# The accumulating blocks of a two-stage expert MLP, with the products of the high parts written ahead of those of the low parts

## The chip, the cores and the metric

The kernel runs on one core of a Trainium2 chip. Its time is the device time of one execution in microseconds (us), the median of several executions. The engines are named as in the profile: PE multiplies matrices (PEld loads its weights), DVE, ACT and POOL work on vectors, SP issues transfers. POOL also issues the indirect transfers (gathers and scatters of rows).

## The reference

Three stages follow each other: a gated linear attention over 4 batches, 8 heads and 768 steps; a routed layer with 8 experts of 384 tokens each; and an MLP with an ELU. For a token `x` of expert `e`:

```python
h = np.maximum(x[mask] @ w1[e], 0.0)
out[mask] = h @ w2[e]
# and then, for all 3072 tokens
h = x @ w_in
g = np.where(h > 0.0, h, alpha * (np.exp(np.minimum(h, 0.0)) - 1.0))
return (g @ w_out)
```

The experts' hidden size is 1024, that of the last MLP is 2048, and a token has 320 numbers. Which expert takes which token is found by a greedy choice over all the scores, which the kernel computes expert after expert.

## The kernel before

The attention comes first. Then eight rounds follow, one for each expert (`NR = 8`), each with its 384 tokens. A round has four kinds of blocks on PE. `P1(r, f)` multiplies the tokens by 128 columns of the first expert matrix (eight blocks); `C1(r, f)` multiplies the result of `P1(r, f)` by the second expert matrix and adds it into three banks named `acc`; `P2(r, f)` does with `w_in` what `P1` does (sixteen blocks); `C2(r, f)` multiplies the result by `w_out` and adds it into three `acc` banks again, one for each 128 tokens. Block `f = 7` of `C1` and block `f = 15` of `C2` end their sums: ACT or DVE then copies the banks out, in `C1` as the input of `P2`, in `C2` as `ot`, which POOL scatters to the rows of the output (line 1375).

For accuracy every operand is a sum of a high and a low part. After a `P` block ACT or DVE writes the high part `gh` (lines 1240, 1093, 1095), and DVE subtracts to get the low part `gl` (lines 1247, 1100), which is therefore ready last. A `C2` block holds, for each of the three banks, three products: `gh` by the high weights (line 1362), `gh` by the low weights (1363) and `gl` by the high weights (1366). A `C1` block holds eight products, in the lines 1315 to 1332.

What stands where on an engine is decided when the program is built. `main` takes the blocks from a list; a `C` block stands some blocks behind its `P` block (`LAG = 3`). Each block is a generator; wherever it yields, side work may be inserted: the router of later rounds, the splitting of the next round's weights, and the transposes that bring the next round's tokens into shape (`prep_x`, line 1176; ACT writes their high part `xh`, and DVE their low part `xl` at line 1184). A planner (`Plan`) keeps an estimated time for each engine and from it decides what is inserted, and whether ACT or DVE takes a copy. Where the first `P1` block of a round comes before the planner has its tokens ready, `main` takes waiting `C2` blocks ahead of it.

One more line stands in the loop of `C2`: in the last round, at `f = 8` and the first bank, `nc.gpsimd.drain()` (line 1369) tells POOL to wait until what it has issued is finished; the planner books 8400 ns for it on POOL. The last `NL = 3` blocks of the last round are one call with `n = 3`.

Of the kernel before, what the change touches and what calls it, by code (L numbers as in the profile page):

```python
# [18 lines left out]
NR, CAP, TK = 8, 384, 384  # L19
# [889 lines left out]
class Mlp:  # L909
# [386 lines left out]
    def C1(self, r, f):  # L1296
        nc, PE, plan = self.nc, self.nc.tensor, self.plan
        A, V = nc.scalar, nc.vector
        if f == 0:
            self.ac = [self.acc.tile([128, 512], F32, name="acc") for _ in range(3)]  # L1300
        h, l, th, tl = self.take(r, 0, f)
        w = self.w2[:, f]
        e = f == 7
        if e:
            yh = self.pool.tile([128, 3, TK], F32R, name="yh", bufs=1)
            yl = self.pool.tile([128, 3, TK], F32R, name="yl", bufs=1)
            for _ in range(2):
                self.es.take(False)[0] = 1
            s = self.pool.tile([128, TK], F32, name="e", bufs=3)[:64]
            ys = self.pool.tile([128, TK], F32, name="e", bufs=3)  # L1310
            self.yst = (yh, yl)
        p = self.ac[2]
        plan.wait(th)
        if f == 0:
            PE.matmul(p[:, :TK], w[:, 512:640], h, start=True, stop=False)
        plan.wait(tl)
        PE.matmul(p[:64, :TK], w[:, 512:576], l, start=False, stop=False)  # L1317
        if f > 0:
            PE.matmul(p[:, :TK], w[:, 512:640], h, start=False, stop=e)  # L1319
        plan.pe(2, TK)  # L1320
        if e:
            A.activation(s, p[64:128, :TK], AF.Copy)
            t1 = plan.on("a", 488)
            V.tensor_tensor(ys[:64], p[:64, :TK], s, op=ALU.add)
            V.tensor_tensor(ys[64:], p[:64, :TK], s, op=ALU.add)
            plan.on("d", 1100, t1)
        for t in range(2):
            p = self.ac[t][:, :TK]
            c, cl = slice(t * 128, t * 128 + 128), slice(256 + t * 128, 384 + t * 128)
            PE.matmul(p, w[:, c], h, start=f == 0, stop=False)  # L1330
            PE.matmul(p, w[:, cl], h, start=False, stop=False)  # L1331
            PE.matmul(p, w[:, c], l, start=False, stop=e)  # L1332
            plan.pe(3, TK)
            if e:
                A.activation(yh[:, t], p, AF.Copy)  # L1335
                t1 = self.yready[t] = plan.on("a", 491)
                V.tensor_tensor(yl[:, t], p, yh[:, t], op=ALU.subtract)
                plan.on("d", 552, t1)
            else:
                yield  # L1340
        if e:
            A.activation(yh[:, 2], ys, AF.Copy)
            t1 = self.yready[2] = plan.on("a", 524)
            V.tensor_tensor(yl[:, 2], ys, yh[:, 2], op=ALU.subtract)
            plan.on("d", 552, t1)
            yield

    def C2(self, r, f, n=1):
        nc, PE, plan = self.nc, self.nc.tensor, self.plan
        if f == 0:  # L1350
            self.ac = [self.acc.tile([128, 512], F32, name="acc") for _ in range(3)]
        parts = {}
        idx = self.router.res[r][1]
        for t, f in [(t, f + i) for t in range(3) for i in range(n)]:
            if f not in parts:
                parts[f] = self.take(r, 1, f)
            h, l, th, tl = parts[f]
            c = slice(t * 128, t * 128 + 128)
            p = self.ac[t][:, :320]
            plan.wait(th)  # L1360
            wh, wl = self.wo(f)
            PE.matmul(p, h[:, c], wh, start=f == 0, stop=False)  # L1362
            PE.matmul(p, h[:, c], wl, start=False, stop=False)  # L1363
            plan.pe(2, 320)
            plan.wait(tl)
            PE.matmul(p, l[:, c], wh, start=False, stop=f == 15)  # L1366
            plan.pe(1, 320)
            if (r, t, f) == (NR - 1, 0, 8):
                nc.gpsimd.drain()
                plan.on("p", 8400)  # L1370
            if f == 15:
                o = self.pool.tile([128, 320], F32, name="ot", bufs=3)
                self.copy(o, p, 437, 490)
                nc.gpsimd.memset(self.spc, 0.0)
                s = nc.gpsimd.indirect_dma_start(out=self.out, out_offset=bass.IndirectOffsetOnAxis(ap=idx[:, t:t + 1], axis=0),  # L1375
                                                 in_=o, in_offset=None)
                for q in self.scat:
                    self.tc.declare_no_dep(s.ins, q.ins, reason="rows of other tokens")
                self.scat.append(s)
                plan.on("p", 1080)  # L1380
            yield
# [281 lines left out]
```

## Time and profile before

| what | value |
|---|---|
| median of 3 runs | 755.16 us (752.74 to 759.88) |
| profiled execution, its own time | 750.71 us |
| profiled execution, span | 748.9 us |
| PE busy in the span | 702.9 us (94%) |
| DVE busy in the span | 541.3 us (72%) |
| ACT busy in the span | 377.6 us (50%) |
| POOL busy in the span | 186.6 us (25%) |

The span runs from the first to the last instruction of the profiled execution; 1.8 us of its time lie around it. PE's share is that of a modelled end of each matmul, so gaps are better read from the starts of matmuls that follow each other. DRAIN and semaphore instructions are no busy time; they stand under an engine's queue (POOLq, SPq).

### The profile page before, as it was taken

To read this page: it belongs to the slowest core of one execution; us is meant where nothing else is said; L and a number is where in the kernel's file an instruction comes from. 1 tells how busy PE (TensorE), PEld (TensorE's weight loads), DVE (VectorE), ACT (ScalarE), POOL (GpSimd) and SP (SyncE) were. 2 spreads that over 40 slices of the span, in tenths; PEclk is the share of its full clock that TensorE was granted. 3 is DMA by queue.
4 is the path that set the end of the run, shared out by engine and by line. 5 is a ranking of instruction groups with operands and counts; after the bars stand their busy time and mean duration, and the time that the engine had idled before them with its cause. 6 is when DMAs were issued, how large, how long until landed. Compare 5 with 4: busy or idle time off the path is not lost.

```text
span 748.9 us, 17930 instructions
## 1 busy us (share of the span) xinstructions
PE 702.9 (94%) x7274; PEld 639.3 (85%) x7274; DVE 541.3 (72%) x1592; ACT 377.6 (50%) x804; POOL 186.6 (25%) x242
## 2 busy tenths in 40 slices
PE   7889888837999999999999999999999999999997
PEld 4656666626989999999999999999999999999997
DVE  8687888887898968965896698569868833851442
ACT  5455445435365725842772366256527743752443
POOL 5666655235111401210301120112022220001001
PEclk9899999957999999999999999999999999999999
DMA  7777968236002301400320230022013321100000
GB/s 280 237 231 226 251 212 261 51 109 214 18 1 85 124 1 51 131 28 1 103 80 28 85 93 5 27 85 98 1 30 109 112 88 45 36 1 26 1 2 27
DMA packets 22436, 67.31 MB, mean 90 GB/s; under 512 B 3536, under 2 KB 7632, under 8 KB 22352
## 3 DMA queue, kind: packets, MB, share of 16 engines
q1 hardware_dynamic: 14240, 35.12, 15.4%
q0 software_dynamic: 8064, 30.94, 12.4%
q8 instruction: 57, 0.93, 0.5%
q14 instruction: 27, 0.22, 0.1%
q10 hardware_dynamic: 48, 0.10, 0.0%
HBM read 58.28 MB, written 7.86 MB: 88 GB/s over the span
## 4 chain that ended last, share of the span: by engine, by line
PE 73%; issue 11%; DVE 9%; ACT 3%; POOL 2%; DMA 1%; POOLq 0%; SPq 0%; ACTq 0%; DVEq 0%
PE ph L1223 30%; PE acc L1362 6%; PE acc L1366 6%; PE acc L1363 6%; PE acc L1330 3%; PE acc L1332 3%; PE acc L1331 2%; PE pO L381 2%; PE pR L395 2%; PE pX L464 2%; PE acc L1317 1%; PE acc L1319 1%; PE pX L450 1%; PE pr L807 1%; PE pO L365 1%
## 5 line engine op out<-in xcount | busy, mean ns | idle before, releaser
L1276 DVE SCALAR_TENSOR_TENSOR e<-e,ph 128x384 f32<-128x384 f32 x128 | 70.3, 550 | 50.4 <-ACT e L1273 49.7
L1272 ACT ACTIVATE e<-ph 128x384 f32<-128x384 f32 x128 | 62.5, 488 | 79.4 <-PE ph L1223 74.3
L1223 PE MATMUL ph<-yh,wih 128*128 128x384 f32 x256 | 89.1, 348 | 0.7 <-DVE xl L1184 0.4
L1240 ACT ACTIVATE gh<-ph 128x384 fp32r<-128x384 f32 x64 | 31.3, 491 | 114.0 <-PE ph L1223 89.1
L1223 PE MATMUL ph<-yh,wil 128*128 128x384 f32 x256 | 86.1, 337 | 0.0
L1375 POOL DMA_INDIRECT out_dram<-ot,idx x24 | 24.0, 998 | 210.8 <-ACT ot L1093 207.8
L1100 DVE TENSOR_TENSOR gl<-e,gh 128x384 fp32r<-128x384 f32 x128 | 70.9, 561 | 1.8 <-ACT gh L1093 0.3
L1273 ACT ACTIVATE e<-e 128x384 f32<-128x384 f32 x128 | 67.3, 526 | 4.0
L1362 PE MATMUL acc<-woh,gh 128*128 128x320 f32 x216 | 68.3, 316 | 0.0
L1247 DVE SCALAR_TENSOR_TENSOR gl<-ph,gh 128x384 fp32r<-128x384 f32 x64 | 35.2, 552 | 45.5 <-ACT gh L1240 45.3
L1366 PE MATMUL acc<-woh,gl 128*128 128x320 f32 x216 | 66.9, 310 | 0.5 <-DVE gl L1100 0.5
L1363 PE MATMUL acc<-wol,gh 128*128 128x320 f32 x216 | 66.8, 309 | 0.0
L1223 PE MATMUL ph<-yl,wih 128*128 128x384 f32 x256 | 66.0, 338 | 0.0
L1093 ACT ACTIVATE gh<-e 128x384 fp32r<-128x384 f32 x96 | 49.0, 514 | 11.4 <-DVE e L1276 11.1
L1366 PE MATMUL acc<-woa,gl 128*128 128x320 f32 x168 | 52.4, 312 | 0.9 <-DVE gl L1100 0.9
L1362 PE MATMUL acc<-woa,gh 128*128 128x320 f32 x168 | 52.8, 314 | 0.0
L1223 PEld LDWEIGHTS ph<-yh,wih 128*128 128x128 f32 x256 | 48.1, 188 | 4.8 <-ACT yh L1335 4.1
L1363 PE MATMUL acc<-wob,gh 128*128 128x320 f32 x168 | 51.8, 308 | 0.0
L1223 PEld LDWEIGHTS ph<-yh,wil 128*128 128x128 f32 x256 | 48.1, 188 | 0.0
L1104 POOL DMA_INDIRECT stg<-in_w1a_dram,wi x16 | 15.7, 983 | 123.3 <-DVE wi L845 119.0
L1223 PEld LDWEIGHTS ph<-yl,wih 128*128 128x128 f32 x256 | 46.1, 188 | 0.0
L1223 PE MATMUL ph<-xh,w1h 128*128 128x384 f32 x128 | 44.6, 349 | 0.1
(290 smaller groups left out, 2041.4 us busy)
## 6 DMA issues: line engine op xcount, KB each, us to landing
vk<-in_vk_dram SPq DMA_DIRECT2D x24, 484.0 KB, 5.4
qk<-in_qk_dram SPq DMA_DIRECT2D x20, 320.0 KB, 5.5
cx<-in_win_dram SPq DMA_DIRECT2D x8, 512.0 KB, 5.1
xd<-x SPq DMA_DIRECT2D x48, 80.0 KB, 3.4
wx<-in_wout_dram SPq DMA_DIRECT2D x9, 320.0 KB, 3.0
cx<-in_wout_dram SPq DMA_DIRECT2D x5, 448.0 KB, 4.1
qk<-in_qk_dram SPq DMA_DIRECT2D x4, 512.0 KB, 6.1
cx<-in_win_dram SPq DMA_DIRECT2D x4, 256.0 KB, 5.7
```

The source lines that it names most:

```text
L1093: self.nc.scalar.activation(out, x, AF.Copy)
L1100: self.nc.vector.tensor_tensor(out, x, y, op=ALU.subtract)
L1223: PE.matmul(p, w, x, start=k == 0, stop=k == 7)
L1240: nc.scalar.activation(h, p, AF.Relu)
L1247: nc.vector.scalar_tensor_tensor(l, p, 0.0, h, op0=ALU.max, op1=ALU.subtract)
L1272: nc.scalar.activation(e, p, AF.Relu, scale=-1.0)
L1273: nc.scalar.activation(e, e, AF.Exp, scale=-1.0)
L1276: nc.vector.scalar_tensor_tensor(e, e, -1.0, p, op0=ALU.add, op1=ALU.max)
L1362: PE.matmul(p, h[:, c], wh, start=f == 0, stop=False)
L1363: PE.matmul(p, h[:, c], wl, start=False, stop=False)
L1366: PE.matmul(p, l[:, c], wh, start=False, stop=f == 15)
L1375: s = nc.gpsimd.indirect_dma_start(out=self.out, out_offset=bass.IndirectOffsetOnAxis(ap=idx[:, t:t + 1], axis=0), in_=o, in_offset=None)
```

## The change

In `C1`, the blocks `f = 0` to `6` now write five products with `gh` (lines 1316, 1318, 1319 of the changed program), a yield, the three with `gl` (1324, 1325), a yield, and return. In `C2`, the blocks `f = 0` to `14` that are called with `n = 1` write six products with `gh` over the three banks (1371, 1372), with yields after the fourth and the sixth, then the three with `gl` (1379), a yield, and return. The closing blocks (`f = 7`, `f = 15`) and the last call with `n = 3` keep the old order. The products themselves, 5730 matmuls in the program, are the same.

The early return of `C2` stands ahead of the line that drains POOL, and that line asks for `f = 8`; in the call with `n = 3`, `f` is 13, 14 or 15. The changed program has no such DRAIN left; the closing ones at the program's end (line 1659 before, 1689 now) are in both.

```diff
@@ C1
         p = self.ac[2]
         plan.wait(th)
-        if f == 0:
-            PE.matmul(p[:, :TK], w[:, 512:640], h, start=True, stop=False)
+        if not e:
+            q = [x[:, :TK] for x in self.ac]
+            PE.matmul(q[2], w[:, 512:640], h, start=f == 0, stop=False)
+            for t in range(2):
+                PE.matmul(q[t], w[:, t * 128:t * 128 + 128], h, start=f == 0, stop=False)
+                PE.matmul(q[t], w[:, 256 + t * 128:384 + t * 128], h, start=False, stop=False)
+            plan.pe(5, TK)
+            yield
+            plan.wait(tl)
+            for t in range(2):
+                PE.matmul(q[t], w[:, t * 128:t * 128 + 128], l, start=False, stop=False)
+            PE.matmul(q[2][:64], w[:, 512:576], l, start=False, stop=False)
+            plan.pe(3, TK)
+            yield
+            return
         plan.wait(tl)
         PE.matmul(p[:64, :TK], w[:, 512:576], l, start=False, stop=False)
-        if f > 0:
-            PE.matmul(p[:, :TK], w[:, 512:640], h, start=False, stop=e)
+        PE.matmul(p[:, :TK], w[:, 512:640], h, start=False, stop=e)
@@ C2
         parts = {}
+        if n == 1 and f < 15:
+            h, l, th, tl = self.take(r, 1, f)
+            wh, wl = self.wo(f)
+            plan.wait(th)
+            q = [(x[:, :320], slice(t * 128, t * 128 + 128)) for t, x in enumerate(self.ac)]
+            for t, (p, c) in enumerate(q):
+                PE.matmul(p, h[:, c], wh, start=f == 0, stop=False)
+                PE.matmul(p, h[:, c], wl, start=False, stop=False)
+                plan.pe(2, 320)
+                if t == 1:
+                    yield
+            yield
+            plan.wait(tl)
+            for p, c in q:
+                PE.matmul(p, l[:, c], wh, start=False, stop=False)
+            plan.pe(3, 320)
+            yield
+            return
         idx = self.router.res[r][1]
```

On PE, the first `C2` block of the first round. Before (a row names the line, the operation and what it writes from what; a bracket names whom it waits for):

```order
L1223 MATMUL ph<-yl,wis 128x384
L1362 MATMUL acc<-woa,gh 128x320 [waits DVE_49]
L1363 MATMUL acc<-wob,gh 128x320
L1366 MATMUL acc<-woa,gl 128x320 [waits DVE_49]
L1362 MATMUL acc<-woa,gh 128x320
L1363 MATMUL acc<-wob,gh 128x320
```

Now:

```order
L1223 MATMUL ph<-yl,wis 128x384
L1371 MATMUL acc<-woa,gh 128x320 [waits DVE_49]
L1372 MATMUL acc<-wob,gh 128x320
L1371 MATMUL acc<-woa,gh 128x320
L1372 MATMUL acc<-wob,gh 128x320
L1371 MATMUL acc<-woa,gh 128x320
L1372 MATMUL acc<-wob,gh 128x320
L1379 MATMUL acc<-woa,gl 128x320 [waits DVE_49]
L1379 MATMUL acc<-woa,gl 128x320 x2
```

Six products stand between the block's start and its first use of `gl`, where two stood.

On PE, the passage from the first round to the second. `L1176` transposes the third part of the next tokens, and the first `ph<-xh` row opens the second round. Before (twelve `C2` products between the two, of which the first four and the last stand here):

```order
L1176 MATMUL ph<-ident,xg 128x128 [waits DMASW5_49]
L1176 MATMUL ph<-ident,xg 128x128
L1176 MATMUL ph<-ident,xg 128x128 [waits Activation_49]
L1362 MATMUL acc<-woh,gh 128x320
L1363 MATMUL acc<-wol,gh 128x320
L1366 MATMUL acc<-woh,gl 128x320
L1362 MATMUL acc<-woh,gh 128x320 [waits Activation_49]
...
L1366 MATMUL acc<-woh,gl 128x320
L1223 MATMUL ph<-xh,w1h 128x384 [waits Activation_49]
```

Now:

```order
L1393 MATMUL acc<-wol,gh 128x320
L1396 MATMUL acc<-woh,gl 128x320
L1176 MATMUL ph<-ident,xg 128x128 [waits DMASW5_49]
L1176 MATMUL ph<-ident,xg 128x128 x2
L1223 MATMUL ph<-xh,w1h 128x384 [waits Activation_49]
L1223 MATMUL ph<-xh,w1l 128x384
```

All `C2` products now stand ahead of the third transposes, and the round's first product, which waits for ACT's copy of them, stands directly behind.

On DVE, the same passage, from the low part of block 14 to the last low part of the next tokens (`u`, `D`, `Lm`, `a_1148` belong to the router). Before, with eight rows of the router left out:

```order
L1100 TENSOR_TENSOR gl<-e,gh 128x384 [waits Activation_49]
L714 TENSOR_SCALAR u<-b 128x24 [waits DVE_49]
...
L1100 TENSOR_TENSOR w1s<-stg,w1s 64x4x128 [waits DMASW2_49,Activation_49]
L1100 TENSOR_TENSOR gl<-e,gh 128x384 [waits Activation_49]
L1100 TENSOR_TENSOR w1s<-stg,w1s 64x4x128 [waits Activation_49]
L1184 TENSOR_TENSOR xl<-ph,xh 128x3x128 [waits Activation_49] x3
```

Now, with the same eight rows left out:

```order
L1100 TENSOR_TENSOR gl<-e,gh 128x384 [waits Activation_49]
L1100 TENSOR_TENSOR w1s<-stg,w1s 64x4x128 [waits DMASW2_49,Activation_49]
L1100 TENSOR_TENSOR gl<-e,gh 128x384 [waits Activation_49]
L714 TENSOR_SCALAR u<-b 128x24 [waits DVE_49]
...
L1100 TENSOR_TENSOR w1s<-stg,w1s 64x4x128 [waits Activation_49]
L1184 TENSOR_TENSOR xl<-ph,xh 128x3x128 [waits Activation_49]
L1184 TENSOR_TENSOR xl<-ph,xh 128x3x128 [waits PE_49,Activation_49]
L1184 TENSOR_TENSOR xl<-ph,xh 128x3x128 [waits Activation_49]
```

The low part of block 15 moved ahead of the router's rows; the three `xl` rows stay last.

## Rows read from the trace of the kernel before

**Rows 1.** The page, part 1: busy time, share of the span, instructions.

```profile
PE 702.9 (94%) x7274; PEld 639.3 (85%) x7274; DVE 541.3 (72%) x1592; ACT 377.6 (50%) x804; POOL 186.6 (25%) x242
```

**Rows 2.** Windows of the rounds: window, length, busy per engine, clock, DMA share, GB/s.

```profile
200.00:225.00 25.00, 24.50 (x165) 22.55 (x163) 20.82 (x67) 13.94 (x30) 3.61 (x4) 1.00 0.00 1
225.00:290.00 65.00, 64.17 (x436) 59.89 (x435) 52.65 (x182) 32.93 (x70) 11.41 (x14) 1.00 0.18 61
640.00:700.00 60.00, 60.00 (x371) 59.47 (x369) 27.72 (x56) 26.83 (x56) 4.54 (x8) 1.00 0.06 20
```

**Rows 3.** The page, part 5: busy, mean ns | idle before, and its releaser.

```profile
L1366 PE MATMUL acc<-woh,gl 128*128 128x320 f32 x216 | 66.9, 310 | 0.5 <-DVE gl L1100 0.5
L1366 PE MATMUL acc<-woa,gl 128*128 128x320 f32 x168 | 52.4, 312 | 0.9 <-DVE gl L1100 0.9
```

**Rows 4.** Timeline of PE, first `C2` block of round one: start, duration, idle before.

```profile
212.04 0.31 PE L1362 MATMUL acc<-woa,gh 128*128 128x320 f32 x1
212.19 0.30 PE L1363 MATMUL acc<-wob,gh 128*128 128x320 f32 x1
212.99 0.41 PE L1366 MATMUL acc<-woa,gl 128*128 128x320 f32 x1 [0.50 <-DVE gl L1100]
213.24 0.30 PE L1362 MATMUL acc<-woa,gh 128*128 128x320 f32 x1
```

**Rows 5.** Timeline of PE, first `C2` block of round two.

```profile
285.56 0.30 PE L1363 MATMUL acc<-wob,gh 128*128 128x320 f32 x1
286.23 0.42 PE L1366 MATMUL acc<-woa,gl 128*128 128x320 f32 x1 [0.36 <-DVE gl L1100]
```

**Rows 6.** Timeline of PE, from round one to round two.

```profile
251.97 0.49 PE L1176 MATMUL ph<-ident,xg 128*128 128x128 f32 x3
252.22 0.40 PE L1362 MATMUL acc<-woh,gh 128*128 128x320 f32 x1
...
252.89 0.31 PE L1363 MATMUL acc<-wol,gh 128*128 128x320 f32 x1
253.66 0.42 PE L1366 MATMUL acc<-woh,gl 128*128 128x320 f32 x1 [0.47 <-DVE gl L1100]
...
254.80 0.34 PE L1223 MATMUL ph<-xh,w1h 128*128 128x384 f32 x1
...
255.65 0.62 PE L1223 MATMUL ph<-xl,w1h 128*128 128x384 f32 x2
```

**Rows 7.** Timeline of ACT, same passage.

```profile
252.50 0.49 ACT L1093 ACTIVATE xh<-ph 128x384 fp32r<-128x384 f32 x1 [0.28 <-PE ph L1176]
254.12 1.32 ACT L1093 ACTIVATE ot<-acc 128x320 f32<-128x320 f32 x3 [1.13 <-PE acc L1366]
```

**Rows 8.** Timeline of DVE, same passage.

```profile
254.13 1.47 DVE L1184 TENSOR_TENSOR xl<-ph,xh 128x384 fp32r<-128x384 f32 x3
```

**Rows 9.** Windows: DVE alone around the passage: window, length, busy, clock, DMA.

```profile
240.00:256.00 16.00, 14.74 (x49) 1.00 0.46 158
```

**Rows 10.** Timeline of POOL, last round.

```profile
684.49 0.97 POOL L1375 DMA_INDIRECT out_dram<-ot,idx  x1 [0.22 <-issue]
692.54 0.09 POOL L1374 MEMSET spc<- 1x1 f32 x1 [7.09 <-issue]
...
745.01 0.97 POOL L1375 DMA_INDIRECT out_dram<-ot,idx  x1 [0.26 <-ACT ot L1093]
```

**Rows 11.** Instructions of lines 1369 and 1659: ns min/median/max, first and last start.

```profile
L1369 POOLq DRAIN  x1: 8925/8925/8925, 683.5 to 683.5; - x1
...
L1659 POOLq EVENT_SEMAPHORE  x4: 17/17/17, 748.2 to 748.8; - x4
L1659 POOLq DRAIN  x3: 51/102/2892, 744.8 to 748.6; - x3
```

**Rows 12.** Windows behind the last scatter of round seven, and of round eight.

```profile
685.46:692.46 7.00, 7.00 (x42) 6.92 (x41) 1.21 (x3) 1.48 (x3) 0.00 (x0) 1.00 0.06 23
745.98:748.90 2.92, 0.00 (x0) 0.00 (x0) 0.00 (x0) 0.00 (x0) 0.00 (x0) 0.66 0.15 56
```

## The prediction

> **What bounds the kernel now.** I read the busy shares first, then the busy times by stage, then the costliest groups of instructions with the idle time ahead of them, and last the timelines of the places where PE waits and of the program's end.
>
> PE is busy for 94% of the span [rows 1]. In the rounds it is busier still: 24.50 of 25.00 us, 64.17 of 65.00, and 60.00 of 60.00 in the windows shown, at a granted clock of 1.00, that is 2.4 GHz [rows 2]. So the rounds last as long as PE's matmuls take, and the change leaves their number and shapes alone. What an order of products can save is idle time of PE. The groups that read the low part `gl` in `C2` show all of it that is due to them: 0.5 and 0.9 us, every time waiting for DVE's subtraction [rows 3]. The reader should see how small that is against 748.9 us of span: fewer waits of this kind can bring a microsecond or so.
>
> The end of the program has another bound. After PE's last product POOL scatters three tiles, and then the closing chain runs: POOL's DRAIN, semaphores, the end [rows 10, 11].
>
> **The reordered products.** Starts tell more than the modelled ends. A `C2` product normally follows its predecessor after 0.15 us (212.04 to 212.19) [rows 4]. In round one's first `C2` block the first use of `gl` comes 0.80 us after the product ahead of it, which loses 0.65, and the next follows after 0.25 instead of 0.15, which loses 0.10: 0.75 us together [rows 4]. In round two the same place has 0.67 instead of 0.15, that is 0.52, and by the same pattern 0.10 behind it: 0.62 us [rows 5]. With six high products ahead of the first low one there are 6 x 0.147 = 0.88 us of cover from the block's start. In round one `gl` was there by 212.99, 0.95 us after the block's start at 212.04, so the cover takes the wait nearly whole; in round two it came 0.67 + 0.15 = 0.82 us after the start, so it takes all. The third wait, 253.66 - 252.89 = 0.77 us [rows 6], is in block 15, which keeps its order.
>
> The other `C1` and `C2` blocks win nothing, since nothing waits in them. That products with equal operands now stand further apart costs nothing either: every product loads its weights anew, before and after (7274 loads for 7274 products) [rows 1]. The side work that is inserted at the yields stands some products earlier or later; it brings the same instructions. On POOL three token gathers of the last round now stand ahead of its weight gathers. Each takes about a microsecond (the scatters' 0.97) [rows 10], on an engine that is busy for 3.61 of 25 us [rows 2], so I cost that at nothing; without that slack it would be 3 us for whoever waits for the weights. SP issues the same transfers in the same order.
>
> **The passage from round one to round two** is where the written order changes in an unwanted way. Before, the third transposes start at 251.97, twelve `C2` products follow, and round two's first product starts at 254.80 [rows 6]. ACT copies the transposes' result at 252.50 for 0.49 us, well inside that [rows 7]. Now nothing stands between them. The copy was done 252.99 - 251.97 = 1.02 us after the transposes' start; PE itself was free after 0.25 (252.22); so 0.77 us are uncovered. Two copies of `ot` of 1.32 / 3 = 0.44 us each now stand ahead of it on ACT [rows 7] and can add about 0.2: a new wait of 1.0 us. Against it, block 15's low part moves ahead of the router's rows on DVE, and its wait goes: 0.62 for the gap and 0.10 behind it would be 0.72, of which I count 0.62. The pause of 0.16 us ahead of the first product with `xl` at 255.65 (four products from 254.80 at 0.174 us would end at 255.50) [rows 6] may go as well. The passage nets +1.0 - 0.6 - 0.2 = +0.2.
>
> Sum of the PE terms: -0.75 - 0.62 + 0.2 = -1.2 us. But DVE was busy for 14.74 of 16.00 us up to this passage [rows 9], and the three `xl` rows, which end at 254.13 + 1.47 = 255.60 [rows 8], release PE's product at 255.65. They stay last in DVE's order behind the same work. A gain that PE made at 212 is therefore lost again here, if DVE comes no earlier. The first block of round two has less of that behind it. I take half of the sum, **-0.6 us**, with bounds of -2.1 (all three waits gone, 0.75 + 0.62 + 0.72, and no new one) and +2.6 (below, rival three).
>
> **The DRAIN that falls out.** The early return skips the one in the last round. Its cost before was hidden: POOL waited in it, with nothing to do until the scatters at the very end. It lasted 8925 ns from 683.5 [rows 11], and POOL's next instruction came at 692.54; the scatter ahead of it ended at 684.49 + 0.97 = 685.46 [rows 10]. So the DRAIN took 7.0 us past the end of the last scatter. The closing DRAIN of line 1659 took 2892 ns from 744.8, until 747.7 [rows 11], that is 1.7 us past the end of its last scatter, 745.01 + 0.97 = 745.98 [rows 10]. Both follow three scatters of the same size. What differs is that the first comes after all gathers and scatters of the program, and the second only after the three issued since. I read the longer time as work for everything issued since the last DRAIN. Without the first, the closing one has to do it, now on the path that sets the end: it would last until 745.98 + 7.0 = 753.0. Before, POOL's last semaphores started at 748.2 and the span ended at 748.9, 0.7 later [rows 11]; so the end moves to 753.7, **+4.8 us**. Bounds: 0, if the 7.0 us belonged to its place in the program, and 8.9 - 2.9 = 6.0, if the whole difference of the two durations comes on top.
>
> The row shows DVE busy for 1.21 of the 7.00 us behind round seven's last scatter, and not at all behind the last one [rows 12]. If POOL stood still for as long as DVE worked there, at most 1.2 of the 7.0 would be gone at the end, and the term would be +3.6. The Trainium skill (SBUF — State Buffer, section "SBUF: two separate sides") says that DVE in some modes shuts POOL out of a shared pair of ports, so that POOL cannot write descriptors; the 17% of DVE time in that window bear out little of it here, and I keep 4.8.
>
> **Sum.** -0.6 + 4.8 = +4.2 us on the profiled execution: 750.71 + 4.2 = 754.9. That execution lies 4.45 us under the median of the runs shown, and my forecast is for such a median: 755.16 + 4.2 = 759.4 us, 0.6% slower.
>
> **Rivals.** *One, 70%: as above.*
>
> *Two, 15%: the end does not grow.* The DRAIN's 7.0 us were due to where it stood (PE, DVE and ACT at work beside it), and the closing one still takes 1.7 us past the last scatter. For it: only one such DRAIN is in the trace, so that its growth with issued transfers is read from two points. Against it: the three scatters ahead of it are of the kind that the closing DRAIN handled in 1.7 us, and the neighbours explain at most 1.2 us. Then only the PE terms are left: 755.2 - 0.6 = 754.6, faster by less than 0.1%. It decides at 1.7 + 0.6 us past the last scatter: a closing DRAIN shorter than that makes the kernel faster than before.
>
> *Three, 11%: DVE's and ACT's order costs PE more than it saves.* At the passage to round two the twelve products from 252.22 to 254.80 [rows 6] no longer cover anything; if `xh` and `xl` come as late as before, by the clock, their 2.6 us stand open. With no gain elsewhere this is 4.8 + 2.6 = +7.4: 762.6. For it: DVE's 14.74 of 16.00 us. Against it: ACT waited for the transposes and was not late itself (idle 0.28 us ahead of the copy) [rows 7].
>
> *Four, 4%: the waits go everywhere and the end does not grow:* -2.1, or 753.1.
>
> A measurement of this kernel tells about 1% (7.5 us) from no change; the three runs shown differ by 7.1. One lies inside for most of its runs' spread (759.4 against 762.7), as do two and four; three ends at the border. That makes 83% within 1%, 14% slower by more, 3% faster by more. The range goes from 753.5, which takes in rival two less a microsecond, to 763.5, rival three and a microsecond.
>
> **What would show it.** In the profile after: no DRAIN of the `C2` line; one DRAIN of the closing line that lasts about 8 us and ends 7 us past the last scatter, and a span that ends some 7.7 us past it instead of 2.9; no idle time ahead of the low products of the two first `C2` blocks; a wait of about 1 us of round two's first product for ACT. A closing DRAIN of 3 us would make the main term wrong; several microseconds of PE idle in the first two rounds would make the other.

## The result, and the profile after

The changed kernel's median is 759.82 us (754.39 to 764.32, 19 runs) against 755.16 before (751.77 to 761.15, 19 runs). The ratio is 1.0061, with a 95% interval from 1.0039 to 1.0083, that is 2.9 to 6.3 us more; the medians differ by 4.7. Its profiled execution took 757.54 us.

The page, part 1, of the kernel after (compare [rows 1]):

```profile
span 755.7 us, 17932 instructions
PE 703.1 (93%) x7274; PEld 641.1 (85%) x7274; DVE 543.1 (72%) x1597; ACT 374.8 (50%) x799; POOL 187.6 (25%) x242
```

PE is as busy as before, 703.1 against 702.9 us, in a span that is 6.8 us longer. So PE was given no more to do; the time is idle. Where it stands, three instants tell: the first product of the rounds, the program's last product, and the end of the span.

The kernel before, timeline of PE at the two instants (start, duration):

```profile
181.35 0.44 PE L1223 MATMUL ph<-xh,w1h 128*128 128x384 f32 x1
...
743.95 0.31 PE L1366 MATMUL acc<-woh,gl 128*128 128x320 f32 x1
```

The same of the kernel after:

```profile
183.81 0.56 PE L1223 MATMUL ph<-xh,w1h 128*128 128x384 f32 x1
...
745.65 0.31 PE L1396 MATMUL acc<-woh,gl 128*128 128x320 f32 x1
```

Ahead of the rounds: 183.81 - 181.35 = +2.5 us. In the rounds: 745.65 - 183.81 = 561.84 against 562.60, -0.8. From the last product to the end: 755.7 - 745.65 = 10.1 against 748.9 - 743.95 = 5.0, +5.1. The first difference is in code that is the same in both. Most of it, 1.8 us, is there by 176 us, as an operation of the router that stands ahead of the rounds shows. Before, then after:

```profile
174.16 0.18 DVE L905 TENSOR_TENSOR ax<-inc,AB 128x24 f32<-128x24 f32 x1
```

```profile
175.99 0.19 DVE L905 TENSOR_TENSOR ax<-inc,AB 128x24 f32<-128x24 f32 x1
```

The granted clock of PE does not account for that part: over the first 180 us its mean was 0.88 before and 0.89 after. What made the difference there stays open. The last 0.6 us fall into a stretch in which PE's clock stood at its lower level, 1.2 GHz, for longer in this execution (third number from the right: the granted clock of the window, as a mean). Before, then after:

```profile
176.00:186.00 10.00, 8.65 (x44) 6.26 (x43) 7.28 (x13) 6.16 (x15) 6.11 (x7) 0.96 0.62 212
```

```profile
176.00:186.00 10.00, 8.24 (x33) 6.03 (x32) 7.19 (x12) 4.84 (x12) 7.05 (x7) 0.76 0.63 206
```

In the eleven profiles of this study the rounds' first product starts between 181.35 and 189.25. So that term changes from one execution to the next, and medians over many should lose it. What is left, -0.8 + 5.1 = +4.3, is near their +4.7.

The end, after (POOL's last scatter, and the DRAINs of the closing line; compare [rows 10] and [rows 11]):

```profile
746.71 0.97 POOL L1405 DMA_INDIRECT out_dram<-ot,idx  x1 [0.26 <-ACT ot L1093]
```

```profile
L1689 POOLq EVENT_SEMAPHORE  x4: 17/17/17, 755.0 to 755.6; - x4
L1689 POOLq DRAIN  x3: 45/102/8468, 746.5 to 755.5; - x3
```

The closing DRAIN lasts 8468 ns where it lasted 2892, and ends at 746.5 + 8.5 = 754.9, 7.3 us past the last scatter's end (747.7). The semaphores that end the program start at 755.0 instead of 748.2.

What POOL's first semaphore waited for is not the same in both. SP has closing instructions of its own, which start when the last scatter's data has landed (at 747.50 before; the trace after shows no landings, and SP starts there at 749.22). Up to POOL's first semaphore, before, then after:

```profile
L1659 SPq EVENT_SEMAPHORE  x9: 27/28/28, 747.5 to 748.0; - x9
L1659 SPq DRAIN  x2: 7/7/7, 748.1 to 748.1; - x2
```

```profile
L1689 SPq EVENT_SEMAPHORE  x9: 28/28/28, 749.2 to 749.7; - x9
L1689 SPq DRAIN  x2: 7/7/7, 749.8 to 749.8; - x2
```

Before, POOL's DRAIN was over at 747.67, and SP, done at 748.15, came last. After, SP was done at 749.85 and the DRAIN came last, at 754.94. SP is done 0.65 us behind the landing in all ten profiles that show it, and a DRAIN's time is hidden behind it for that long. Behind as many transfers as here the closing DRAIN ends 5.74 us behind the landing (experiments below), and 5.74 - 0.65 = 5.09 us is near the 5.10 that the end grew by.

The waits of PE in the rounds, after, by total:

```profile
PE ph L1223 <- DVE xl L1184: 1.0, 1, 1.0
PE ph L1223 <- ACT xh L1093: 0.7, 1, 0.7
PE acc L1316 <- DVE w L1100: 0.3, 1, 0.3
```

No wait for `gl` is left, where three stood (1.3 us in that view). Two others are new or longer. One is at the passage to round two, where the third transposes now stand directly ahead of the round's first product (compare [rows 6] and [rows 7]). PE, then ACT:

```profile
255.30 0.49 PE L1176 MATMUL ph<-ident,xg 128*128 128x128 f32 x3
256.53 0.44 PE L1223 MATMUL ph<-xh,w1h 128*128 128x384 f32 x1 [0.74 <-ACT xh L1093]
```

```profile
255.32 0.77 ACT L1093 ACTIVATE ot<-acc 128x320 f32<-128x320 f32 x2
255.96 0.52 ACT L1093 ACTIVATE xh<-ph 128x384 fp32r<-128x384 f32 x1
```

By the starts, 256.53 - 255.30 - 0.25 = 0.98 us stand open: ACT finishes two copies of `ot` first, then copies `xh`. The other wait is in round two, 1.00 us of a `P2` product for DVE's `xl`:

```profile
313.56 0.49 PE L1176 MATMUL ph<-ident,xg 128*128 128x128 f32 x3
315.05 0.44 PE L1223 MATMUL ph<-yh,wih 128*128 128x384 f32 x1 [1.00 <-DVE xl L1184]
```

### The profile page after: what moved, and what is told of

Read it like the earlier page. It is cut to its first block, busy times and chain, and to the rows that moved or that the text cites. A ratio compares the mean times of both kernels' runs of the same rounds, so it can differ in the third digit from the quotient of the medians.

```text
span 755.7 us, 17932 instructions
## 1 busy us (share of the span) xinstructions
PE 703.1 (93%) x7274; PEld 641.1 (85%) x7274; DVE 543.1 (72%) x1597; ACT 374.8 (50%) x799; POOL 187.6 (25%) x242
## 4 chain that ended last, share of the span: by engine, by line
PE 72%; issue 11%; DVE 9%; ACT 3%; DMA 2%; POOL 2%; POOLq 0%; SPq 0%; ACTq 0%; DVEq 0%
PE ph L1223 31%; PE acc L1379 6%; PE acc L1371 6%; PE acc L1372 6%; PE acc L1324 2%; PE acc L1319 2%; PE acc L1318 2%; PE pO L381 2%; PE pX L464 2%; PE pR L395 2%; PE acc L1316 1%; PE acc L1325 1%; DMA vk<-in_vk_dram 1%; PE pr L807 1%; DMA qk<-in_qk_dram 1%
## 5 line engine op out<-in xcount | busy, mean ns | idle before, releaser
L1371 PE MATMUL acc<-woh,gh 128*128 128x320 f32 x186 | 56.3, 313 | 0.0
L1372 PE MATMUL acc<-wol,gh 128*128 128x320 f32 x186 | 55.6, 309 | 0.0
L1093 ACT ACTIVATE gh<-e 128x384 fp32r<-128x384 f32 x89 | 45.1, 515 | 16.7 <-DVE e L1276 16.7
L1372 PE MATMUL acc<-wob,gh 128*128 128x320 f32 x168 | 50.1, 308 | 0.0
L1223 PE MATMUL ph<-yh,wis 128*128 128x384 f32 x128 | 43.6, 341 | 0.0
L1223 PE MATMUL ph<-yl,wis 128*128 128x384 f32 x128 | 43.3, 338 | 0.0
```

The source lines that it names most:

```text
L1093: self.nc.scalar.activation(out, x, AF.Copy)
L1223: PE.matmul(p, w, x, start=k == 0, stop=k == 7)
```

## The experiments

Two theories stood against each other. The first: the order of the products gains about half a microsecond, and the lost DRAIN costs some 5 us at the end. The second: the new order costs the time by its new waits, and the DRAIN is a bystander.

**The changed order with its DRAIN.** Added to the early return of `C2`:

```diff
             plan.pe(3, 320)
+            if (r, f) == (NR - 1, 8):
+                nc.gpsimd.drain()
+                plan.on("p", 8400)
             yield
```

> The changed order of products with the DRAIN put back at the same place (last round, block 8 of C2). Theory (the lost DRAIN makes the time, the order of products gains about half a microsecond): the closing DRAIN falls from 8468 ns back to about 2900 ns, the end stands 4.9 us behind the last product instead of 10.0, and the time is 755.2 - 0.6, a ratio of 0.998 to 1.000 to the kernel before. Rival (the order of products, with its new wait at the passage to round two, makes the time): the closing DRAIN shortens and the time stays near 759.8, ratio 1.006.

Measured: 755.17 us against 753.42 (12 and 17 runs), ratio 1.0008 (0.9982 to 1.0033). Its DRAINs, the one put back and the closing ones:

```profile
L1382 POOLq DRAIN  x1: 8930/8930/8930, 687.8 to 687.8; - x1
...
L1692 POOLq DRAIN  x3: 51/102/2895, 749.0 to 752.8; - x3
```

The closing one is back at 2.9 us, the end 753.1 - 748.14 = 5.0 us behind the last product. So the order alone does not make the time: the interval holds 1.000 and leaves the rival's 1.006 out.

**The old order without its DRAIN,** measured twice, because the first result lay over what its own trace showed.

```diff
             if (r, t, f) == (NR - 1, 0, 8):
-                nc.gpsimd.drain()
                 plan.on("p", 8400)
```

> The kernel before without its DRAIN in the last round, order of products untouched. Theory: the closing DRAIN lasts about 8.4 us, 7 us past the last scatter, and the time is 755.2 + 4.9 = 760.1, ratio 1.0065 (1.004 to 1.009). Rival (the order makes the time): ratio 1.000.

> The kernel before without its DRAIN once more, since its first measurement (ratio 1.011, 1.0078 to 1.0143) lies over the 5.1 us that the end grew by in its profile. Theory (only the end grows, the rest was the spread of six runs): ratio 1.004 to 1.009, and the end stands 10.1 us behind the last product. Rival (without the DRAIN something ahead of the rounds is slower as well): ratio 1.009 or more again.

Measured first: 761.17 against 753.42, ratio 1.0110 (1.0078 to 1.0143), from 6 runs, above the range expected; again: 759.15 against 754.19, ratio 1.0060 (1.0039 to 1.0080), from 12. The profiled end grew by the same in both, and by as much as in the changed kernel. Last product and closing DRAINs of the first:

```profile
749.67 0.31 PE L1366 MATMUL acc<-woh,gl 128*128 128x320 f32 x1
```

```profile
L1658 POOLq DRAIN  x3: 45/102/8467, 750.5 to 759.5; - x3
```

759.8 - 749.67 = 10.1 us again. Taking the DRAIN away with the old order gives the whole slowdown. The second measurement agrees with the 5.1 us of the end (0.7%); of the first, even the lower edge of the interval (0.78%) lies 0.1% above that. I take this excess for the spread of six runs in the stages ahead of the rounds; it was not examined further, and so stays open.

**One half of the order at a time,** both with the DRAIN. Only `C1` is changed in the first, where `C2` goes its old way; only `C2` in the second, where the early path of `C1` is taken out and the DRAIN put back as above. Against the changed kernel:

```diff
-        if n == 1 and f < 15:
+        if False:
```

```diff
-        if not e:
...
-            return
+        if f == 0:
+            PE.matmul(p[:, :TK], w[:, 512:640], h, start=True, stop=False)
...
             plan.pe(3, 320)
+            if (r, f) == (NR - 1, 8):
+                nc.gpsimd.drain()
+                plan.on("p", 8400)
             yield
```

> Only the blocks of C1 are reordered; C2 and its DRAIN are as before. Theory: no wait for a low part stood in C1, so from the first product of the rounds to the last it takes 562.6 us, as before, within 0.7; the three waits for gl in C2 (1.3 us in the view of waits) are still there; the end stands 4.9 us behind the last product. Rival (C1's order matters): the rounds become shorter or longer by over 1 us.

> Only the blocks of C2 are reordered, with the DRAIN kept; C1 is as before. Theory: the waits for gl at the starts of rounds one and two go (0.75 + 0.62 us by the starts of the matmuls), and the passage to round two gets a wait of about 1 us for ACT's copy; the rounds take 561.5 to 562.6 us against 562.6. Rival (C1's order brings what the rounds gained, 0.8 us): 562.6 or more. The end stands 4.9 us behind the last product.

One profiled time of each, 754.49 and 755.14 us, tells nothing of half a microsecond; the trace has to. Measured from the first product of the rounds to the last: 561.98 us for `C1` alone, within what was expected, and 560.51 for `C2` alone, 1 us below it, against 562.60. But the old order itself took 561.40 without its DRAIN, so this stretch is too coarse: its first `C1` block waits for weights, 0.9 us in the kernel before and 0.3 in the changed one, and that changes from profile to profile. From round one's first `P2` product on, the old order agrees with itself:

| order of the products | us from round one's first P2 product to the last product |
|---|---|
| old, six profiles | 538.0 to 538.2 |
| C1 alone | 747.70 - 209.04 = 538.7 |
| C2 alone | 748.35 - 211.24 = 537.1 |
| both (changed kernel; with the DRAIN put back) | 537.9; 537.4 |

`C2`'s order gains about 1 us, `C1`'s loses about half of one, and together they gain 0.3 to 0.8 against the kernel before (538.2). A single profile stands behind each half, and the two profiles with both differ by 0.5 us themselves, so `C1`'s half microsecond is an indication and not shown; most of it (0.3) lies in rounds three to eight, where no wait is in view, and its cause stays open. With `C1` alone the three waits for `gl` are all there, with `C2` alone none:

```profile
PE acc L1396 <- DVE gl L1100: 1.3, 3, 0.5
```

```profile
PE ph L1223 <- DVE xl L1184: 1.0, 1, 1.0
PE ph L1223 <- ACT xh L1093: 0.7, 1, 0.7
```

**Who sets the time of the passage to round two.** The changed order with its DRAIN, but old blocks 12 to 14 in round one:

```diff
-        if n == 1 and f < 15:
+        if n == 1 and f < 15 and not (r == 0 and f > 11):
```

> The changed order with the DRAIN put back, except that blocks 12 to 14 of C2 in round one keep the old order, so that twelve C2 products stand again between the third transposes and round two's first product. From round one's first P2 product to round two's took 73.36 us in the kernel before and 72.96 with the changed order and the DRAIN. Theory (the new wait at the passage costs PE what I counted, and PE sets the pace): the wait for ACT's copy, 0.7 us in the view of waits, goes, and the stretch takes 72.0 to 72.6. Rival (DVE sets the time of the passage): the wait goes, another for DVE's gl or xl takes its place, and the stretch takes 72.9 to 73.4. In both the ratio to the kernel before lies between 0.997 and 1.001.

Measured: ratio 1.0001 (0.9972 to 1.0030), and 72.94 us for the stretch against 72.96. The wait for ACT went, and one for DVE took its place:

```profile
PE ph L1223 <- DVE xl L1184: 1.0, 1, 1.0
PE acc L1399 <- DVE gl L1100: 0.5, 1, 0.5
```

The first of the two lines is the wait in round two, which stays. The run alone does not settle who sets the time, since its edit also put block 15's low part back behind the router's rows on DVE: a gain went together with the wait. The rows of DVE's last `xl` and of PE's first product with it do. Changed kernel, then this run:

```profile
255.72 1.47 DVE L1184 TENSOR_TENSOR xl<-ph,xh 128x384 fp32r<-128x384 f32 x3
257.33 0.53 PE L1223 MATMUL ph<-xl,w1h 128*128 128x384 f32 x2
```

```profile
258.26 1.01 DVE L1184 TENSOR_TENSOR xl<-ph,xh 128x384 fp32r<-128x384 f32 x2
259.32 0.62 PE L1223 MATMUL ph<-xl,w1h 128*128 128x384 f32 x2
```

In this run PE's product follows 259.32 - 259.27 = 0.05 us behind the end of `xl`, as it did in the kernel before (255.60 to 255.65); in the changed kernel 257.33 - 257.19 = 0.14. Counted from round one's first `P2` product DVE is done after 49.4 us in both. So the rival holds here: DVE sets the time of that passage, and without its wait for ACT the changed kernel could have gained some 0.1 us there (an estimate from these rows), not 0.98.

**What a DRAIN's time depends on.** All three kernels have the old order. First a DRAIN in every round:

```diff
-            if (r, t, f) == (NR - 1, 0, 8):
+            if (t, f) == (0, 8):
                 nc.gpsimd.drain()
+            if (r, t, f) == (NR - 1, 0, 8):
                 plan.on("p", 8400)
```

> The kernel before with a DRAIN at block 8 of C2 in every round, not in the last alone; some 11 indirect transfers then lie between two DRAINs. Theory A (a DRAIN works off what POOL issued since the last one, by the two points so far 7.02 us for 85 transfers and 1.69 us past the last scatter for 3, that is 0.065 us each): the DRAINs of the eight rounds last about 0.5 to 2.2 us beyond POOL's instruction ahead of them, none 7. Theory B (the first DRAIN in the rounds pays a fixed price): the first lasts about 7 us, the others under 2. Theory C (a price of its own in every DRAIN that follows a long stretch without one): each lasts about 7 us. The closing one stays at 1.7 us past the last scatter in all three.

Then the only DRAIN moved ahead of all gathers and scatters, to the start of `run`:

```diff
             if (r, t, f) == (NR - 1, 0, 8):
-                nc.gpsimd.drain()
                 plan.on("p", 8400)
...
         plan = self.plan
+        self.nc.gpsimd.drain()
         fill, routes = self.start(first)
```

> The kernel before with its DRAIN moved from the last round to the start of the rounds' stage, when none or only a few of the 88 indirect transfers have been issued. Theory A (work for the transfers issued since): the closing DRAIN lasts about 8.4 us and ends 7.0 to 7.3 us past the last scatter, the end stands 10.1 us behind the last product. Theory B (the first DRAIN pays a fixed price): the early one lasts some microseconds, and the closing one ends 1.7 us past the last scatter.

And DRAINs in rounds two, six and eight:

```diff
-            if (r, t, f) == (NR - 1, 0, 8):
+            if r in (1, 5, 7) and (t, f) == (0, 8):
                 nc.gpsimd.drain()
+            if (r, t, f) == (NR - 1, 0, 8):
                 plan.on("p", 8400)
```

> The kernel before with DRAINs at block 8 of C2 in rounds two, six and eight, so that some 25, 46 and 14 indirect transfers lie between them. Counted from the landing of the last transfer ahead of it, a DRAIN took 0.16 us behind 3 transfers, 0.49 behind 11, 0.57 behind 13, 0.61 behind 14, 5.50 behind 85 and 5.74 behind 88. Theory (time per transfer issued since the last DRAIN, between the 0.041 us of the short stretches and the 0.065 of the long ones): about 1.0 to 1.6 us behind 25 and 1.9 to 3.0 behind 46. Rival (a threshold between 14 and 85, beyond which the DRAIN takes 5 us more): 0.5 to 1.0 behind 25, and either under 2 or over 5 behind 46. The closing one 0.16, and the end 5.0 us behind the last product.

The single times were 757.47, 759.98 and 755.53 us, and the end 5.0, 10.1 and 5.0 us behind the last product. With a DRAIN in each round they lasted between 3590 and 8906 ns, and ended 3.6 to 5.5 us past the end of the scatter or gather ahead (1.7 in the last round), more than my theory's 0.5 to 2.2: I had counted from the end of POOL's instruction, not from the landing of its data. The early DRAIN lasted 0.8 us and saved nothing, the closing one 8.5, which speaks against a price that only the first one pays:

```profile
L1659 POOLq DRAIN  x3: 45/102/8465, 749.0 to 757.9; - x3
```

Counted from the landing, all agree. For instance the first of the three in the last run, with the gather ahead of it (its start, and its time to landing):

```profile
L1369 POOLq DRAIN  x1: 6699/6699/6699, 308.3 to 308.3; - x1
...
L1104 POOL DMA_INDIRECT xg<-xd,idx x1: 946/946/946, 310.0 to 310.0; - x1
...
DMA to landing us min/median/max: 3.9/3.9/3.9
```

Landed at 313.9, drained at 308.3 + 6.7 = 315.0: 1.07 us behind 25 transfers, by the trace's finer figures. All of them:

| transfers since the last DRAIN | us from the last landing to the DRAIN's end | us each |
|---|---|---|
| 3 | 0.16 | 0.05 |
| 11 | 0.49 to 0.50 | 0.045 |
| 13, 14 | 0.57, 0.61 | 0.044 |
| 25 | 1.07 | 0.043 |
| 46 | 1.92 | 0.042 |
| 85 | 5.50 | 0.065 |
| 88 | 5.74 | 0.065 |

Up to 46 transfers a DRAIN costs about 0.04 us for each; between 46 and 85 it grows faster, (5.50 - 1.92) / 39 = 0.09. Behind 25 and 46 transfers the DRAINs came out at the lower edge of what was expected, and the rival's figures are missed by little at 25 (1.07, where it said 0.5 to 1.0) and met at 46 (1.92, where it said under 2). A fixed price does not fit the rows, and a jump of 5 us is more than the whole rise from 46 to 85, which is 3.6; a smaller jump between the two stays open. The step from 85 to 88, 0.08 us each, looks more like a slope. The time since the last DRAIN is not what counts: 11 transfers took 0.50 us with 241 us behind them and 0.49 with some 70. Gathers and scatters are counted alike here; no run separates them. Why the slope rises was not tried.

## Why the prediction was right

**The DRAIN's term** was forecast at +4.8 and measured at +5.1. The closing DRAIN took over the work of the lost one, as rival two denied: 7.0 us past the last scatter forecast, 7.3 measured. Of the missing 0.3, 0.24 are the three scatters more that it has to cover (88 against 85: 5.74 against 5.50). My split of the old closing DRAIN was incomplete: of its 1.7 us past the scatter, 1.5 are the scatter's landing (745.01 + 2.5 = 747.5 of 747.7), and 0.16 are the DRAIN's own. The sum was not hurt, since the landing is in both.

One step of the sum was taken without a reason, and that it holds is luck. The old DRAIN ended at 747.7 and POOL's first semaphore started at 748.2; I let the 0.5 us between them go. With them the end would have moved by 753.0 - 747.7 = 5.3. They do go, because SP was last before, so that the old closing DRAIN did not set the end; I had read the end as set by the DRAIN in both.

That a scatter's row on POOL ends ahead of its data agrees with the Trainium skill (Perfetto Trace Analysis, "DMA Instruction — SWDGE (GPSIMD)"): the profiler's end is that of writing the descriptors. The row lasts 0.97 us, the data lands after 2.5.

**DVE beside the DRAIN** was given at most 1.2 us. The runs show none of it: behind the last scatter no engine had anything to do, and the DRAIN was no shorter. The window between the scatter's end and the DRAIN's end, after (compare [rows 12]):

```profile
747.68:754.94 7.26, 0.00 (x0) 0.00 (x0) 0.00 (x0) 0.00 (x0) 0.00 (x0) 0.71 0.06 23
```

So what the Trainium skill (SBUF — State Buffer, "SBUF: two separate sides") says of DVE shutting POOL out shows no part in this DRAIN's time.

**The waits for `gl`** went as worked out. In round one the first low product starts 0.23 us after the high one ahead of it, 0.08 more than 0.15, where I left 0.07 uncovered:

```profile
214.05 0.31 PE L1371 MATMUL acc<-woa,gh 128*128 128x320 f32 x1
...
214.78 0.30 PE L1372 MATMUL acc<-wob,gh 128*128 128x320 f32 x1
215.01 0.71 PE L1379 MATMUL acc<-woa,gl 128*128 128x320 f32 x3
```

Block 15's wait went too, by the move in DVE's order.

**The passage to round two** was forecast to expose 1.0 us and exposed 0.98. That it hardly counts, because DVE sets the time there, was my reason for taking half of the sum, and DVE's rows bear it out. The wait of 1.0 us for `xl` in round two I had not seen; 0.4 of it stood there before. Whatever `C1`'s order loses I had at nothing. Together PE's terms came to -0.3 to -0.8, and I had taken -0.6. That this fits is in part luck: the half was a guess, worked out from no row, and two of the terms that make up the measured sum are not in mine.

**Rival three** found its mechanism (DVE late at the passage) but not its price: of its 2.6 us 0.98 stood open, and DVE's last `xl` came 49.4 us behind round one's first `P2` product instead of 49.8, so the stretch up to round two's became shorter (73.36 us before, 73.09 in the changed kernel, 72.96 with the DRAIN).

## What to carry to other kernels

Ask of an early return what else it returns from: here a line for another engine sat in the same loop, and only its absence on POOL's queue showed in the time. A wait that costs nothing in the middle of a program (POOL idle for 50 us behind it) may be work that some later wait, on the path that sets the end, has to do otherwise; look for two waits of the same kind with unlike durations. And where PE is busy for 99% of a stage, count the waits that a new order can take away before trying it: 1.3 us in the view of waits, 2.1 by the starts of the products, was all there was. At the end of a program, look which engine comes last: a DRAIN that another engine's closing work covers costs nothing until it is longer than that.

## What the runs showed that was not expected

The DRAIN of POOL scales with the indirect transfers issued since the last one, 0.04 us each up to 46 and more beyond, on top of the landing of the last. Long before the end it is hidden; one such DRAIN in the last round's block 8, alone or with others in earlier rounds, leaves 0.16 us of its own for the closing one, and these are hidden behind SP's 0.65 us. By the table some 14 transfers (0.61 us) would still be hidden there; that is an estimate, no run ended so. And the start of the rounds moved by 8 us between profiles (181.35 to 189.25 us), more than the whole effect. The end, between 4.98 and 4.99 us with a DRAIN in the last round and 10.08 without in every profile, was the steadier gauge.
